# One attention output in every step, and the convolution between the second and third score tile

## Chip, cores and metric

The kernel runs on 1 core of one Trainium2 chip. Time is device microseconds of one execution; a few runs of each kernel are timed, beside runs of the kernel before on the same chip.

## The reference, cut

```python
# q, k, v: (8, 8, 576, 64); block causal attention (blocks of 64), then a gated linear unit
scores = np.where(mask, scale * (q @ k^T), -1e9)        # mask: block_i >= block_j
attn   = exp(scores - max) / (sum + 1e-9);  a = attn @ v
x      = a.transpose(0, 2, 1, 3).reshape(B, S, 512)      # (8, 576, 512)
gate   = sigmoid(causal_conv5(x, conv_w));  val = x @ w_val
out    = (gate * val) @ w_out                            # float32
# ... cut
```

Of the kernel before, what the change touches and what calls it, by code (L numbers as in the profile page):

```python
# [10 lines left out]
def kernel(  # L11
# [27 lines left out]
    B, H, S, D = q.shape  # L39
    NT = B * 4  # L40

    def mm(**kw):
        tc.keep_in_program_order(nc.tensor.matmul(**kw))  # L43
# [126 lines left out]
    def first_q(h, i):  # L170
        return 2 * i + 1 + h

    def scores(t, part):
        b, n = divmod(t, 4)
        if part == 0:
            pts[t] = ptp.tile([128, 2880], fp16, tag="pt", name="pt")
        pt = pts[t]
        hs = (slice(0, 64), slice(64, 128))
        qT = [qkT[b][hs[h], n, 0, :] for h in range(2)]
        kT = [qkT[b][hs[h], n, 1, :] for h in range(2)]  # L180

        def full(ps, h, i, lo):
            f = 64 * first_q(h, i)
            mm(out=ps[:, h, lo:lo + S - f], lhsT=kT[h][:, f - 64:f + 64], rhs=qT[h][:, f:S],
               start=True, stop=True, skip_group_check=True)

        def ex(o, src, w):
            nc.scalar.activation(out=pt[:, o:o + w], in_=src, func=AF.Exp, bias=0.0,  # L188
                                 scale=0.125)

        if part == 0:
            ps = psS.tile([128, 2, 512], fp32, tag="S")
            full(ps, 0, 0, 0)
            full(ps, 1, 0, 0)
            full(ps, 1, 3, 448)
            ex(0, ps[:, :, :], 1024)
            ps = psS.tile([128, 2, 512], fp32, tag="S")
            full(ps, 0, 1, 0)
            full(ps, 1, 1, 0)
            full(ps, 0, 3, 384)  # L200
            full(ps, 1, 2, 320)
            ex(1024, ps[:, :, :], 1024)
            return
        q4 = [x.rearrange("d (j x) -> d j x", x=64) for x in qT]
        if part == 1:
            ps = psS.tile([128, 2, 512], fp32, tag="S")
            full(ps, 0, 2, 0)
            mm(out=ps[64:128, 1, 0:256], lhsT=kT[1][:, 0:64], rhs=q4[1][:, 1:8:2, :],
               start=True, stop=True, skip_group_check=True)
            for i in range(4):  # L210
                f = 64 * (2 * i + 1)
                mm(out=ps[0:64, 1, 64 * i:64 * i + 64], lhsT=kT[1][:, f:f + 64],
                   rhs=qT[1][:, f:f + 64], start=True, stop=True, skip_group_check=True)
            nc.scalar.activation(  # L214
                out=pt[:, 2048:2560].rearrange("p (h x) -> p h x", h=2),
                in_=ps[:, :, 0:256], func=AF.Exp, bias=0.0, scale=0.125)
            return
        ps = psS.tile([128, 2, 512], fp32, tag="S")
        mm(out=ps[64:128, 0, 0:320], lhsT=kT[1][:, 0:64], rhs=q4[1][:, 0:9:2, :],
           start=True, stop=True, skip_group_check=True)  # L220
        for i in range(5):
            f = 128 * i
            mm(out=ps[0:64, 0, 64 * i:64 * i + 64], lhsT=kT[0][:, f:f + 64],
               rhs=qT[0][:, f:f + 64], start=True, stop=True, skip_group_check=True)
        ex(XO, ps[:, 0, 0:320], 320)

    def p_cols(pt, h, i, lo, hi):
        o = TOF[h][i] + 64 * (lo - first_q(h, i))
        return pt[:, o:o + 64 * (hi - lo)]
# [52 lines left out]
    def pv(t):  # L282
        b, n = divmod(t, 4)
        pt = pts.pop(t)
        v16, vd, vz = vts[b]
        xb = xbs[b % NXB]
        rb = rp.tile([128, 2, 9, 32], fp32, tag="rb")
        vec.stream_shuffle(out=rb[:, :, :, :].rearrange("p e j y -> p (e j y)"),
                                 in_=rqs[b % 2][:, :, :].rearrange("p e x -> p (e x)"),
                                 mask=[n] * 32)  # L290
        for part, (lo, hi) in enumerate(((0, 5), (5, 9))):
            nb = hi - lo
            x = psG.tile([128, nb, 64], fp32, tag="G")
            todo = []
            for h in range(2):
                hs = slice(64 * h, 64 * h + 64)
                jobs = []
                for i in range(4):
                    a = max(lo, first_q(h, i))
                    if a < hi:  # L300
                        jobs.append(dict(out=x[hs, a - lo:, :],
                                         lhsT=v16[:, 9 * n + 5 * h + i, :],
                                         rhs=p_cols(pt, h, i, a, hi)))
                if h == 1:
                    for i in range(4):
                        j = 2 * i + 1
                        if lo <= j < hi:
                            jobs.append(dict(out=x[hs, j - lo, :], lhsT=vd[:, n, i, :],
                                             rhs=pt[:, YO + 64 * i:YO + 64 * i + 64]))
                    i0, m = ((0, 3), (3, 2))[part]  # L310
                    jobs.append(dict(out=x[hs, 2 * i0 - lo:nb:2, :],
                                     lhsT=vz[:, n, 5, :],
                                     rhs=pt[:, XO + 64 * i0:XO + 64 * (i0 + m)]))
                else:
                    for i in range(5):
                        if lo <= 2 * i < hi:
                            jobs.append(dict(out=x[hs, 2 * i - lo, :],
                                             lhsT=vz[:, n, i, :],
                                             rhs=pt[:, XO + 64 * i:XO + 64 * i + 64]))
                todo.append(jobs)  # L320
            for z in range(max(len(x_) for x_ in todo)):
                for x_ in todo:
                    if z < len(x_):
                        mm(start=(z == 0), stop=(z == len(x_) - 1), skip_group_check=True,
                           **x_[z])
            vec.tensor_tensor(
                out=xb[:, n, 4 + 64 * lo:4 + 64 * hi].rearrange("p (j e y) -> p j e y", e=2, y=32),
                in0=x[:, :, :].rearrange("p j (e y) -> p j e y", e=2),
                in1=rb[:, :, lo:hi, :].rearrange("p e j y -> p j e y"),
                op=ALU.mult)  # L330
# [87 lines left out]
    for t in range(NT + LAG):  # L418
        b, r = divmod(t, 4)
        m = t - LAG  # L420
        hb = (t + 3) // 2 if t % 2 else t // 2 + 1
        tr = [(hb, part) for part in ((1, 2), (0,))[t % 2]] if hb < 2 * B else []
        if t == 0:
            tr.insert(0, (1, 0))
        if t < NT:
            scores(t, 0)
        if t % 2 == 0:
            load_pair(t // 2 + 3)
        if r == 0 and b < B:
            load_v(b)  # L430
        if t in (2, 3, 6, 7):
            weights(t // 4, t % 2 * 2)
        if r == (2 if b else 1) and b < B:
            cast_v(b)
        if t <= 4:
            conv_weights(t - 1)
        if proj:
            project(*proj.pop(0))
        if r == 0 and 1 <= b <= B:
            den(b - 1)  # L440
        if m < 0 and tr:
            trans(*tr.pop(0))
        for n in range(2):
            if r == 3 and 1 <= b <= B:
                pv(4 * b - 4 + n)
            if r == 0 and 2 <= b <= B + 1:
                pv(4 * b - 6 + n)
            if n == 0 and t < NT:
                if 0 <= m:
                    scores(t, 1)  # L450
                    scores(t, 2)
                else:
                    scores(t, 1)
                    if tr:
                        trans(*tr.pop(0))
        if m < 0 and t < NT:
            scores(t, 2)
        if r == 1 and 1 <= b <= B:
            spread(b - 1)
        if 0 <= m < NT:  # L460
            gate(*divmod(m, 4))
        if tr:
            trans(*tr.pop(0))
        if 0 <= m < NT:
            val(*divmod(m, 4))
            u, i = divmod(m, 8)
            if i == 3:
                proj.extend((u, j) for j in range(4))
            if i == 7:
                proj.extend((u, j) for j in range(4, 9))  # L470
        if tr:
            trans(*tr.pop(0))
        if proj:
            project(*proj.pop(0))
    while proj:
        project(*proj.pop(0))


# [1 line left out]
_INS = ['q', 'k', 'v', 'moe_w_val', 'moe_conv_w', 'moe_w_out']  # L480
_OUTS = [((8, 576, 512), 'float32')]
# [25 lines left out]
```

## The kernel before: what the change touches

One step `t` handles the scores of one *pair* of heads. A batch has four pairs, so four steps; step `t` is step `r = t % 4` of batch `b = t // 4`. The convolution and value product of a pair run nine steps later (`m = t - 9`).

```python
stg = ...bufs=4   # staging of loads
psS = ctx.enter_context(tc.tile_pool(name="psS", bufs=2, space=PSUM))   # score tiles
psG = ctx.enter_context(tc.tile_pool(name="psG", bufs=4, space=PSUM))   # all other small PSUM tiles
# scores(t, 0): two score tiles, exp of 128x1024 each; scores(t, 1): third, exp 128x512; scores(t, 2): fourth, exp 128x320
# den(b):   88 small matmuls -> dn, then the reciprocal on DVE
# spread(b): eight 32x288 copies of the reciprocals, on POOL (half on DVE for batch 0)
# pv(t):    shuffle on DVE, attention output matmuls -> two psG tiles x, two multiplies on DVE -> xb
# gate:     two times five matmuls -> cv, tanh on ACT;   val: two times four matmuls -> vp, multiply on DVE
# project:  four matmuls -> ot, ACT copies to ob, and ACT issues the store:
        nc.scalar.copy(out=ob[:, :], in_=ot[:, :])
        nc.scalar.dma_start(out=out2d[...], in_=ob[:, :])

    LAG = 9
    for t in range(NT + LAG):
        ...
        if t < NT:
            scores(t, 0)
        ...                                   # loads and casts
        if proj:
            project(*proj.pop(0))
        if r == 0 and 1 <= b <= B:
            den(b - 1)
        ...
        for n in range(2):
            if r == 3 and 1 <= b <= B:
                pv(4 * b - 4 + n)
            if r == 0 and 2 <= b <= B + 1:
                pv(4 * b - 6 + n)
            if n == 0 and t < NT:
                if 0 <= m:
                    scores(t, 1)
                    scores(t, 2)
                ...
        if r == 1 and 1 <= b <= B:
            spread(b - 1)
        if 0 <= m < NT:
            gate(*divmod(m, 4))
        ...                                   # transposes, val, transposes, project
```

The softmax here doesn't subtract the row's maximum and nothing guards it: scores larger than these inputs give would overflow.

## Time and profile before

| | before |
|---|---|
| time, median of 3 (range) | 264.78 us (262.64 to 264.83) |
| span of the profiled run | 261.9 us |
| PE / DVE / ACT / POOL busy | 85 / 57 / 53 / 44% |
| one steady batch | 28.09 us (29.34 us with one store more); once 34.76 us |

Lines of the page of the kernel before: busy microseconds of each engine, then busy tenths of PE and the granted TensorE clock in 40 slices of the span.

```profile
PE 222.4 (85%) x3064; PEld 153.8 (59%) x3064; DVE 149.2 (57%) x297; ACT 138.3 (53%) x233; POOL 116.0 (44%) x168
...
PE   0698986888989998997698989899989997999993
...
PEclk9997799779999999999599999999999999999999
```

PE is the engine to shorten. Past the start (the first 59 us) only one slice has a low clock (5, near 124 to 131 us). The list of PE's waits in the kernel before (total, times, longest):

```profile
PE ps L43 <- ACT pt L188: 14.5, 29, 3.6
...
PE x L43 <- DVE ri L56: 2.0, 5, 1.0
...
PE cv L43 <- DVE xb_68 L56: 1.7, 3, 0.7
PE cv L43 <- DVE xb_67 L56: 1.4, 2, 0.7
```

`ps` are the score tiles. There are two buffers; the third and fourth tile of a step wait until an exponential has emptied one. PE's timeline in one plain step of the kernel before (start, length, group, idle time before it and its releaser):

```profile
150.47 0.51 PE L43 MATMUL ps<-qkT 64*128 64x256 f16 x6
151.39 0.34 PE L43 MATMUL ps<-qkT 64*64 64x320 f16 x6 [0.41 <-ACT pt L188]
151.66 1.40 PE L43 MATMUL cv<-xb_67,diag 128*128 128x288 f16 x10
```

and around the second attention output and the convolution in the step with the denominators:

```profile
165.04 0.54 PE L43 MATMUL x<-pt,t 128*64 128x256 f16 x8 [0.27 <-DVE ri L56]
...
166.35 0.90 PE L43 MATMUL cv<-xb_67,diag 128*128 128x288 f16 x6 [0.67 <-DVE xb_68 L56]
```

The gap of 0.41 us comes back in three of the four steps of a batch, the two lower ones once per batch. What stands between the second and third tile differs: a projection alone (1.1 us from start to start, gap of 0.41 us at 88.52 us), one attention output alone (1.0 us, 0.41 us at 94.21 us), and in the denominator step the denominators with one attention output. Three batches in a row, by window of the kernel before (length, then busy time and instructions of PE, PEld, DVE, ACT, POOL, then PEclk, DMA share, GB/s):

```profile
75.41:103.50 28.09, 25.48 (x381) 17.84 (x381) 17.08 (x34) 16.26 (x28) 14.19 (x21) 1.00 0.93 277
103.50:138.26 34.76, 28.83 (x384) 19.59 (x384) 17.17 (x34) 16.90 (x29) 14.00 (x21) 0.90 0.48 142
138.26:166.35 28.09, 25.61 (x380) 17.85 (x380) 17.07 (x34) 16.29 (x28) 13.99 (x21) 1.00 0.32 81
```

The middle one is 6.7 us longer. ACT's timeline in it shows why: a store in ACT's queue (`ACTq`) is issued 3.6 us after its copy `ob` ended, and the exponentials behind it in the queue wait.

```profile
121.10 0.58 ACT L376 COPY ob<-ot 128x512 f32<-128x512 f32 x1 [2.36 <-PE ot L43]
121.58 1.03 ACT L188 ACTIVATE pt<-ps 128x1024 f16<-128x1024 f32 x1
125.32 0.34 ACTq L377 DMA_DIRECT2D out_dram<-ob  x1
125.71 1.02 ACT L188 ACTIVATE pt<-ps 128x1024 f16<-128x1024 f32 x1 [3.10 <-DMA st<-in_q_dram]
```

The compiled program says what the store waits for. It hands eight DMA semaphores out in turn, to loads and stores alike, and a new DMA waits for the last user of its semaphore. This store got one last used by a q load that was stuck behind the small-packet v load; that load was issued at 115.29 us and landed 10.0 us later, at 125.29, and the store was issued at 125.32:

```
ACT  out_0_dram<-ob_2252      [waits DMAHW2, Activation]
SP   st_2717<-in_q_dram       [waits DMAHW6, DMAHW2]
```

### The profile page before, as it was taken

The numbers are of one execution on the slowest core, as the hardware profiler recorded it, in microseconds if no ns is written. First come the engines' busy times: TensorE is split into PE (matmuls) and PEld (weight loads), VectorE is DVE, ScalarE is ACT, GpSimd is POOL, SyncE is SP. The second block draws the span as 40 slices with busy tenths as digits, with TensorE's granted clock in tenths as the row PEclk, the third lists the DMA queues.
The fourth block names the chain that finished last, engine by engine and source line by source line (L and its number), as shares of the span: only waits on it lengthen the run. The fifth ranks groups of instructions, "written<-read, shape, count | busy, mean of one in ns | idle before, by whom it ended". The sixth has DMA issues, their size and how long they took to land.

```text
span 261.9 us, 7260 instructions
## 1 busy us (share of the span) xinstructions
PE 222.4 (85%) x3064; PEld 153.8 (59%) x3064; DVE 149.2 (57%) x297; ACT 138.3 (53%) x233; POOL 116.0 (44%) x168
## 2 busy tenths in 40 slices
PE   0698986888989998997698989899989997999993
PEld 0465655656765567554475568655665566677661
DVE  2269995934693297527167257932775167458140
ACT  2558695256636655673343775266645760442533
POOL 5354973996986713943009730770029202200000
PEclk9997799779999999999599999999999999999999
DMA  6998688969479696149800290029101210230305
GB/s 196 341 280 217 213 250 215 327 196 300 148 166 348 232 271 236 40 133 282 292 3 3 85 245 14 4 83 241 62 3 40 83 41 3 83 120 4 131 32 200
DMA packets 24875, 40.33 MB, mean 154 GB/s; under 512 B 1797, under 2 KB 11013, under 8 KB 24842
## 3 DMA queue, kind: packets, MB, share of 16 engines
q1 hardware_dynamic: 19648, 30.41, 40.1%
q10 hardware_dynamic: 5194, 9.45, 9.9%
q8 instruction: 24, 0.39, 0.6%
q14 instruction: 9, 0.07, 0.1%
HBM read 30.42 MB, written 9.44 MB: 152 GB/s over the span
## 4 chain that ended last, share of the span: by engine, by line
PE 54%; ACT 16%; DVE 15%; DMA 6%; issue 4%; SPq 1%; POOL 1%; ACTq 0%; DVEq 0%
PE cv L43 14%; ACT pt L188 13%; PE ps L43 9%; PE vp L43 9%; PE ot L43 8%; PE dn L43 5%; PE tr L152 5%; PE x L43 5%; DVE ri L56 4%; DMA st<-in_q_dram 4%; DVE rb L56 4%; DVE qkT L56 3%; DMA st<-in_k_dram 2%; ACT ob L376 2%; DVE xb_68 L56 1%
## 5 line engine op out<-in xcount | busy, mean ns | idle before, releaser
L188 ACT ACTIVATE pt<-ps 128x1024 f16<-128x1024 f32 (+1 forms) x96 | 76.0, 828 | 23.3 <-PE ps L43 19.5
L56 DVE COPY qkT<-tr 128x768 f16<-128x768 f16 (+1 forms) x62 | 49.3, 837 | 52.4 <-PE tr L152 52.3
L43 PE MATMUL ps<-qkT 64*64 64x64 f16 (+10 forms) x608 | 49.8, 256 | 17.7 <-ACT pt L188 14.5
L43 PEld LDWEIGHTS <-qkT 64*64 64x64 f16 (+1 forms) x608 | 24.9, 105 | 45.2 <-issue 38.0
L348 ACT ACTIVATE th<-cv 128x288 f32<-128x288 f32 x64 | 26.2, 410 | 39.1 <-PE cv L43 37.2
L118 POOL CAST t<-st 128x1152 f16<-128x1152 f32 x30 | 34.1, 1143 | 22.5 <-issue 9.8
L56 DVE SCALAR_TENSOR_TENSOR gv<-th,vp 128x288 f16<-128x288 f32 x64 | 27.0, 447 | 26.5 <-PE vp L43 25.9
L376 ACT COPY ob<-ot 128x512 f32<-128x512 f32 x36 | 21.3, 591 | 37.4 <-PE ot L43 36.3
L43 PEld LDWEIGHTS <-diag 128*128 128x128 f16 x320 | 30.4, 100 | 14.2 <-issue 4.1
L43 PE MATMUL ot<-w_out_sb,gv 128*128 128x512 f16 x144 | 35.8, 380 | 0.5
L152 PE MATMUL tr<-ident_59,t 128*128 128x128 f16 x288 | 27.3, 240 | 7.7 <-DVE ident_59 L94 6.5
L43 PE MATMUL x<-pt,t 128*64 128x256 f16 (+3 forms) x384 | 27.9, 258 | 3.3 <-DVE ri L56 2.0
L279 POOL COPY rq_71<-ri 32x288 f32<-32x288 f32 x32 | 13.4, 420 | 35.6 <-DVE ri L56 34.4
L152 PEld LDWEIGHTS <-t 128*128 128x128 f16 x288 | 21.4, 108 | 12.0 <-DVE t L56 6.3
L279 POOL COPY rq_70<-ri 32x288 f32<-32x288 f32 x28 | 11.8, 421 | 36.2 <-DVE ri L56 35.1
L43 PEld LDWEIGHTS <-w_val_sb 128*128 128x128 f16 x256 | 24.3, 98 | 5.5
L214 ACT ACTIVATE pt<-ps 128x512 f16<-128x512 f32 x32 | 19.7, 615 | 14.0 <-PE ps L43 13.9
L43 PEld LDWEIGHTS <-t 128*64 128x64 f16 x384 | 18.9, 113 | 7.4 <-issue 5.0
L131 POOL CAST t<-st 128x2304 f16<-128x2304 f32 x8 | 16.8, 2103 | 11.8 <-DMA st<-in_v_dram 11.5
L43 PEld LDWEIGHTS <-gv 128*128 128x128 f16 x144 | 12.7, 98 | 14.7 <-issue 2.1
L56 DVE RECIPROCAL ri<-dn 128x288 f32<-128x288 f32 x8 | 15.6, 1956 | 9.9 <-PE dn L43 9.9
L43 PE MATMUL cv<-xb_67,diag 128*128 128x288 f16 x120 | 18.0, 299 | 1.7 <-DVE xb_68 L56 1.7
(55 smaller groups left out, 258.5 us busy)
## 6 DMA issues: line engine op xcount, KB each, us to landing
st<-in_q_dram SPq DMA_DIRECT2D x32, 288.0 KB, 4.9
st<-in_k_dram SPq DMA_DIRECT2D x32, 288.0 KB, 5.0
out_dram<-ob ACTq DMA_DIRECT2D x36, 256.0 KB, 2.0
st<-in_moe_w_val_dram SPq DMA_DIRECT2D x2, 512.0 KB, 6.6
st<-in_moe_w_out_dram SPq DMA_DIRECT2D x2, 512.0 KB, 5.6
st<-in_v_dram SPq DMA_DIRECT2D x8, 0.2 KB, 9.4
conv_nat<-in_moe_conv_w_dram ACTq DMA_DIRECT2D x1, 10.0 KB
```

What stands on the lines that cost most here:

```text
L43: tc.keep_in_program_order(nc.tensor.matmul(**kw))
L56: return lambda **kw: tc.keep_in_program_order(f(**kw))
L118: cast(out=t[:, :, :, :], in_=st[:, :, :, :].rearrange("p z c d -> p c z d"))
L131: nc.gpsimd.tensor_copy(out=t[:, :, :], in_=st[:, :, :])
L152: tc.keep_in_program_order(nc.tensor.transpose(out=tr[:, s, :], in_=q16[hb, w][:, c, :, :], identity=ident16[:, :]))
L188: nc.scalar.activation(out=pt[:, o:o + w], in_=src, func=AF.Exp, bias=0.0, scale=0.125)
L214: nc.scalar.activation(out=pt[:, 2048:2560].rearrange("p (h x) -> p h x", h=2), in_=ps[:, :, 0:256], func=AF.Exp, bias=0.0, scale=0.125)
L279: move.tensor_copy(out=rqs[b % 2][r0:r0 + 32, e, :], in_=ri[r1:r1 + 32, :])
L348: nc.scalar.activation(out=th[:, HF * hf:HF * hf + HF], in_=cv[:, :], func=AF.Tanh, bias=0.0, scale=0.5)
L376: nc.scalar.copy(out=ob[:, :], in_=ot[:, :])
```

## The change

The intent: give ACT enough time between the second and the third score tile, by one attention output per step in place of two in every other step, and by the convolution in between. No work is added or removed.

```diff
-        for n in range(2):
-            if r == 3 and 1 <= b <= B:
-                pv(4 * b - 4 + n)
-            if r == 0 and 2 <= b <= B + 1:
-                pv(4 * b - 6 + n)
-            if n == 0 and t < NT:
-                if 0 <= m:
-                    scores(t, 1)
-                    scores(t, 2)
-                else:
-                    scores(t, 1)
-                    if tr:
-                        trans(*tr.pop(0))
-        if m < 0 and t < NT:
+        if 0 <= t - 6 < NT:
+            pv(t - 6)
+        if m < 0:
+            scores(t, 1)
+            if tr:
+                trans(*tr.pop(0))
             scores(t, 2)
         if r == 1 and 1 <= b <= B:
             spread(b - 1)
         if 0 <= m < NT:
             gate(*divmod(m, 4))
+            if t < NT:
+                scores(t, 1)
+                scores(t, 2)
```

## The prediction

> **What bounds it now.** TensorE. The page has PE busy 222.4 of 261.9 us (85%), DVE 57%, ACT 53%; PE is 54% of the chain that ended last. In the timeline the steady stretch repeats per batch of four pairs: from the convolution after a batch's last attention output to the next, 28.09 us (75.4 to 103.5, 138.3 to 166.4), PE busy 25.5. So 2.5 us per batch are PE gaps, regular ones:
> - The third and fourth score tiles need a score buffer (there are two) that an exponential must free. Between second and third tile PE has a projection, one attention output, or nothing; ACT needs 1.8 us for two wide exponentials. PE idles about 0.2 and 0.4 us a step; the list of waits gives 14.5 us in 29 waits.
> - In the denominator step a 1.96 us reciprocal blocks DVE, and two attention outputs fill the four small PSUM buffers: gaps of 0.27 and 0.68 us.
> - Once, at 122 to 126 us, ACT sits 3.1 us: a store in its queue is issued at 125.3 though its copy ended at 121.7. The instruction listing shows that the store reuses a DMA semaphore whose previous user is a q load, itself queued behind the small-packet v load (the wait is put down to that load). PE waits 3.62 us, and the granted clock is then 0.5 until about 131 us (convolution 2.58 us, elsewhere 1.40). That batch takes 34.76 us, 6.7 over its neighbours. This agrees with the Trainium skill, "TensorE: Matmul & The Clock Gate", HAM oscillation: PE gaps over about 3.4 us bring back the half clock.
>
> **The change.** No work is added or removed. Attention outputs go from two per step in two steps of four (7 and 8 steps late) to one in every step (6 late). Convolution (1.24 us of PE from start to start) and attention output (1.05) stand between second and third score tile in every steady step, so ACT has 2.3 us and more for two exponentials. The last two are covered by value product (1.0) and transposes.
>
> **On the critical path** (sums of timeline gaps):
> 1. Score tiles waiting for exponentials after 52 us, without the stall: 8.9 us; I expect 8 gone.
> 2. Denominator steps: 1 us each; a wait of the second convolution half for the reciprocal remains (1.05 plus 0.6 against 2.0 us: 0.4). Net gain 3 us over the kernel.
> 3. The stall: DMA semaphores are handed out in another order; the ninth store now waits for a DMA landed long before. Gain 6.5 us, if no other store falls on a late load; I see none.
> 4. New: the first attention output, at step 6, directly needs the spread reciprocals (done near 37 us) while DVE is full: up to 1.5 us lost, mostly regained in steps 7 and 8. Other new waits: 1 us. The tail keeps its work.
>
> 264.8 - 8 - 3 - 6.5 + 2 = about 249 us. Range 244 to 257. Faster by over 2%: 0.93; within 2%: 0.06; slower: 0.01.
>
> **What would show it.** Score tiles waiting for exponentials down from 14.5 to under 4 us; batch period 26 us or a little less, PE busy time equal; no ACT wait over 2 us on an input load and no half clock after 60 us; in the denominator step one gap of 0.4 us before the second convolution half. Tail equal within 1 us.
>
> **What would make it wrong.** The stall comes back elsewhere, with half clock (+6). PE time that I call busy is partly waiting hidden by modelled ends, so gaps only move. The four small PSUM buffers bring waits for DVE or ACT in every step. Waits like the "issue" one of 1.97 us at 45.5 fall worse in the DMA-heavy start.

## The result, and the profile after

| | before | after |
|---|---|---|
| time, median | 264.42 us (4 runs) | 244.88 us (4 runs, one of them slow, 248.22) |
| ratio | | 0.9268, 95% interval 0.9212 to 0.9324 |
| span of the profiled run | 261.9 us | 242.9 us |
| PE busy | 222.4 us, 85% | 218.9 us, 90% |

A ratio is the mean time of one kernel's fast runs over that of the other's fast runs of the same rounds, so it is not quite the ratio of the medians. The kernel takes 7.3% less time.

The same lines of the page, after:

```profile
PE 218.9 (90%) x3064; PEld 147.1 (61%) x3064; DVE 151.6 (62%) x297; ACT 140.1 (58%) x233; POOL 116.5 (48%) x168
...
PE   0598989897699999999999999999999999999993
...
PEclk9998577999799999999999999999999999999998
```

PE's waits after:

```profile
PE vp L43 <- DVE xb_68 L56: 3.7, 1, 3.7
PE cv L43 <- DVE ri L56: 3.0, 6, 0.5
PE ps L43 <- ACT pt L188: 1.7, 6, 0.4
```

The wait for exponentials of this form fell from 14.5 to 1.7 us, all of it in the first 52 us (those of the third tile's exponential, `pt L214`, went from 0.3 to 0.8 us, also there). A plain step of the kernel after, on PE, has no gap that the view shows:

```profile
143.10 0.61 PE L43 MATMUL ps<-qkT 64*128 64x512 f16 x7
143.64 0.35 PE L43 MATMUL x<-pt,t 128*64 128x256 f16 x4
...
144.47 1.41 PE L43 MATMUL cv<-xb_67,diag 128*128 128x288 f16 x10
145.81 0.28 PE L43 MATMUL ps<-qkT 64*128 64x256 f16 x1
```

The batches by window, after; no one is long now, as no store is held (the middle one has one store more than its neighbours):

```profile
74.07:99.67 25.60, 25.02 (x380) 16.78 (x380) 17.33 (x34) 16.57 (x28) 14.05 (x20) 1.00 0.92 262
99.67:126.40 26.73, 26.06 (x384) 17.09 (x384) 17.38 (x34) 17.04 (x29) 14.10 (x20) 1.00 0.69 220
126.40:152.00 25.60, 25.02 (x380) 16.78 (x380) 17.34 (x34) 16.57 (x28) 14.10 (x20) 1.00 0.35 100
```

Two gaps are left. One is 0.50 us in the denominator step: the second half of the convolution waits for the PSUM slot of the denominators `dn`, which the reciprocal on DVE (`ri`) still reads. PE's timeline of the kernel after shows it:

```profile
125.11 0.79 PE L43 MATMUL cv<-xb_69,diag 128*128 128x288 f16 x5
126.40 0.78 PE L43 MATMUL cv<-xb_69,diag 128*128 128x288 f16 x5 [0.50 <-DVE ri L56]
```

The other, of 3.65 us at 59 us, is new (`vp` in the list of waits). It is the first attention output of batch 1. DVE's timeline after, there:

```profile
54.82 0.81 DVE L56 SCALAR_TENSOR_TENSOR gv<-th,vp 128x288 f16<-128x288 f32 x2
61.32 0.01 DVE L56 LOAD_MASK_SELECT rb<-rq_71  x1 [5.69 <-POOL rq_71 L279]
61.32 0.79 DVE L56 STREAM_SHUFFLE rb<-rq_71 128x576 f32<-128x576 f32 x1
```

DVE waits 5.69 us for POOL's spreading copies, which end at 61.3 us because casts stand before them. Half clock follows for 3.4 us.

Where the 19.0 us of span went. The first matmul of each of the eight denominators is a common mark in both PE timelines; the table has the time between marks.

| stretch | before | after | difference |
|---|---|---|---|
| start to den 0 | 27.85 | 28.08 | +0.23 |
| den 0 to 1 | 14.12 | 16.59 | +2.47 |
| 1 to 2 (new stall in after) | 28.46 | 25.74 | -2.72 |
| 2 to 3 | 28.08 | 25.60 | -2.48 |
| 3 to 4 (store stall in before) | 34.77 | 26.73 | -8.04 |
| 4 to 5 | 28.10 | 25.60 | -2.50 |
| 5 to 6 | 29.34 | 26.72 | -2.62 |
| 6 to 7 | 26.21 | 23.72 | -2.49 |
| 7 to end | 44.97 | 44.12 | -0.85 |

The start is noisy: two other kernels below that are the same program up to denominator 1 reached it at 43.73 and 44.50 us, against 41.97 in before; the kernel after, run again below, reached it at 41.80 us, against 44.67 here. So +2.47 lies within the scatter of the start. The same holds for -2.72: the second profile of the kernel after has 29.35 us there. Denominator 2 was reached at 70.41 and 71.15 us in the two profiles of after, and at 70.43, 70.82 and 73.26 us in before and those two kernels: the start as a whole shows no gain clear of its scatter. The stretch from 3 to 4 has five stores, as that from 5 to 6 has; against that neighbour the store stall costs 34.77 - 29.34 = 5.4 us.

### The profile page after: what moved, and what is told of

Read it like the earlier page. It is cut to its first block, busy times and chain, and to the rows that moved or that the text cites. A ratio compares the mean times of both kernels' runs of the same rounds, so it can differ in the third digit from the quotient of the medians.

```text
span 242.9 us, 7262 instructions
## 1 busy us (share of the span) xinstructions
PE 218.9 (90%) x3064; PEld 147.1 (61%) x3064; DVE 151.6 (62%) x297; ACT 140.1 (58%) x233; POOL 116.5 (48%) x168
## 4 chain that ended last, share of the span: by engine, by line
PE 59%; DVE 12%; DMA 12%; POOL 9%; SPq 4%; issue 2%; ACT 0%; POOLq 0%; DVEq 0%; ACTq 0%
PE cv L43 14%; PE ot L43 13%; PE vp L43 9%; PE ps L43 8%; DMA st<-in_k_dram 7%; PE x L43 7%; DVE qkT L56 5%; DVE ri L56 5%; SPq L46 4%; PE tr L152 4%; DMA st<-in_v_dram 4%; PE dn L43 4%; POOL t L118 3%; POOL rq_71 L279 1%; POOL d L135 1%
## 5 line engine op out<-in xcount | busy, mean ns | idle before, releaser
L43 PE MATMUL ps<-qkT 64*64 64x64 f16 (+10 forms) x608 | 46.2, 259 | 4.1 <-ACT pt L188 1.7
L43 PEld LDWEIGHTS <-qkT 64*64 64x64 f16 (+1 forms) x608 | 21.5, 105 | 28.9 <-issue 20.8
L43 PEld LDWEIGHTS <-diag 128*128 128x128 f16 x320 | 28.8, 98 | 12.7 <-issue 4.1
L152 PE MATMUL tr<-ident_59,t 128*128 128x128 f16 x288 | 27.8, 243 | 8.3 <-DVE ident_59 L94 7.0
L152 PEld LDWEIGHTS <-t 128*128 128x128 f16 x288 | 19.9, 108 | 13.5 <-DVE t L56 6.8
L214 ACT ACTIVATE pt<-ps 128x512 f16<-128x512 f32 x32 | 19.1, 598 | 9.3 <-PE ps L43 7.8
L43 PEld LDWEIGHTS <-t 128*64 128x64 f16 x384 | 18.4, 113 | 9.4 <-issue 7.9
L43 PEld LDWEIGHTS <-gv 128*128 128x128 f16 x144 | 12.7, 98 | 14.8 <-issue 2.1
L43 PE MATMUL cv<-xb_67,diag 128*128 128x288 f16 x120 | 17.4, 289 | 1.0 <-DVE ri L56 1.0
```

Source lines behind the costliest of these rows:

```text
L43: tc.keep_in_program_order(nc.tensor.matmul(**kw))
L152: tc.keep_in_program_order(nc.tensor.transpose(out=tr[:, s, :], in_=q16[hb, w][:, c, :, :], identity=ident16[:, :]))
L214: nc.scalar.activation(out=pt[:, 2048:2560].rearrange("p (h x) -> p h x", h=2), in_=ps[:, :, 0:256], func=AF.Exp, bias=0.0, scale=0.125)
```

## The experiments

Theory A: the plain gain is hidden exponentials, and any PE block of about 1 us between second and third tile does it. Rivals: only one of the two moves matters, or both are needed. Apart from that, the store stall and the new stall have theories of their own.

### Only the convolution moved

```diff
                 if 0 <= m:
+                    gate(*divmod(m, 4))
                     scores(t, 1)
                     scores(t, 2)
...
-        if 0 <= m < NT:
+        if 0 <= m < NT and t >= NT:
             gate(*divmod(m, 4))
```

> Kernel before, with only the convolution moved between second and third score tile; attention outputs stay in pairs in two steps of four. Theory A (any PE block of about 1 us between the tiles hides the exponentials, and pairing the attention outputs costs a second gap in the denominator step): waits of score tiles for exponentials fall under 3 us in total, the denominator step keeps gaps of about 1 us, a batch takes about 26.6 us against 28.1 before and 25.6 after. The instruction listing shows that here the ninth store reuses the DMA semaphore of the v load itself, so an ACT stall of 2 to 3 us comes back at about 120 us. No POOL stall at 59 us, as the attention outputs start as late as before. Time 252 us (248 to 257). Theory B (one attention output per step is what matters, the place of the convolution nothing): waits for exponentials stay over 8 us, time 258 us or more.

Measured: 245.98 us, ratio 0.9274 (0.9223 to 0.9325). After 52 us there is one wait for an exponential, of 1.41 us at 120 us, and it is the store stall that was expected there: the v load was issued at 110.67 us and landed 8.1 us later, at 118.77, and the ninth store, whose copy had ended at 116.32, was issued at 118.80. An earlier store was held as well, for 2.8 us until 81.76 us (the releaser is a q load): PE waits 1.83 us, and den 2 to 3 takes 27.88 us against 25.60 in after. Den 4 to 5 takes 25.89 us (before 28.10, after 25.60); there the convolution waits 0.50 us for the reciprocal and a projection 0.56 us. There is no 3.65 us stall (den 1 to 2: 23.17 us). The absent 3.65 us stall hides in the total what the two held stores cost, so that the total equals that of the kernel after is partly chance; the steady batch is the cleaner measure. There the move of the convolution alone gives 2.21 of 2.50 us, and rival B falls. But the convolution hardly ever stands alone here: a projection, an attention output or the denominators stand beside it (2.2 us from start to start at 133.02 us). In the two steps where it is alone (51.63 and 55.50 us, 1.34 us from start to start) no wait for it is listed; in the second the twelve matmuls of the third and fourth tile take 0.95 us in place of 0.64.

### Only the attention outputs moved

```diff
+            if t < NT:
+                scores(t, 1)
+                scores(t, 2)
             gate(*divmod(m, 4))
-            if t < NT:
-                scores(t, 1)
-                scores(t, 2)
```
(against the kernel after)

> Kernel after, with the convolution put back behind the fourth score tile; one attention output per step stays between second and third tile. Theory A: the attention output (1.05 us of PE) already covers the wait: the score buffer of the third tile is free about 0.5 us after the second tile, that of the fourth about 1.4 us after it. Waits for exponentials stay under 3 us; the 0.50 us gap before the second convolution half in the denominator step goes, because the score tiles then stand between; batch 25.2 to 25.8 us; the POOL stall of 3.65 us at 59 us stays. Time 243 us (240 to 247). Rival C (both blocks are needed): waits for exponentials of 0.4 us in each step without a projection, batch 26.5 us or more, time 249 us or more.

Measured: 246.21 us, ratio 0.9273 (0.9213 to 0.9332). The profiled run was the slow one (249.45 us), with 5.22 us of new stall in place of 3.65; only its steady part is used. Den 4 to 5 takes 25.72 us. The 0.50 us gap in the denominator step is gone except in the last batch, but one of 0.2 us before the value product is left there. And in the step ahead of it, where the attention output stands alone between the tiles, PE still waits for exponentials: 0.41 us in each of the last five batches, and in two of them 0.22 us more. PE's timeline of this run:

```profile
121.52 0.35 PE L43 MATMUL x<-pt,t 128*64 128x256 f16 x4
...
122.64 0.51 PE L43 MATMUL ps<-qkT 64*128 64x256 f16 x6 [0.22 <-ACT pt L188]
123.56 0.34 PE L43 MATMUL ps<-qkT 64*64 64x320 f16 x6 [0.41 <-ACT pt L188]
```

In the two steps where a projection stands there too (1.80 us from start to start at 108.06 us) there is no gap. Rival C falls for the time: each move alone gives nearly the whole steady gain, and the gains don't add. Theory A falls too as it was worded. A block of 1.0 us alone leaves 0.41 us, here and in the kernel before; the convolution's 1.34 us alone leaves 0.3 us at most, and 1.8 us and more leaves none. One move was enough because most steps already had another block in that place.

### The store stall: another semaphore

```diff
         nc.scalar.dma_start(out=out2d[...], in_=ob[:, :])
+        if (u, j) == (0, 7):
+            nc.scalar.dma_start(out=spare[0:1, 0:64], in_=ob[0:1, 0:64])
```
(against the kernel before)

> Kernel before, with one store of 256 bytes into an unused tile added behind the eighth output store, so that the ninth reuses the DMA semaphore of the eighth store and no longer that of the late q load. Theory: the ACT wait of 3.1 us and the PE wait of 3.6 us at 122 to 126 us and the half clock after them go, the batch falls from 34.8 to 29.3 us, time 264.4 - 5.4 = 259 us (257.5 to 260.5), ratio 0.980. Rival (the ACT store issue is late because the DMA rings are full of small v packets, not because of the semaphore): the stall stays, time 264.

Measured: 264.25 us, ratio 0.9966 (0.9904 to 1.0027): no gain. But the wait is another one. ACT's timeline of this run:

```profile
121.48 0.58 ACT L377 COPY ob<-ot 128x512 f32<-128x512 f32 x1 [1.95 <-PE ot L43]
...
125.00 0.40 ACTq L378 DMA_DIRECT2D out_dram<-ob  x1
125.44 1.02 ACT L189 ACTIVATE pt<-ps 128x1024 f16<-128x1024 f32 x1 [2.45 <-DMA out_dram<-ob]
```

The releaser is now the eighth store (`out_dram<-ob`), whose semaphore the ninth got, and that store had landed late as well (issued at 117.46 us, 7.5 us to landing, against a median of 2.0 us over the kernel before), at 124.96 us; the ninth was issued at 125.00. So the run misses: I had picked a semaphore whose user was late too, and it doesn't tell the theories apart by time. The change of the releaser speaks for the semaphore.

### The store stall: the store from another queue

```diff
-        nc.scalar.dma_start(out=out2d[...], in_=ob[:, :])
+        q = nc.gpsimd if (u, j) == (0, 8) else nc.scalar
+        q.dma_start(out=out2d[...], in_=ob[:, :])
```
(against the kernel before)

> Kernel before, with only the ninth output store issued from POOL's queue in place of ACT's. The run with the spare store left the stall, but its releaser changed from the q load to the eighth store, as the semaphore given to the ninth store did. Theory: the stall is ACT's queue held by that one store; with the store elsewhere ACT goes on, the PE wait of 3.6 us and the half clock go, the batch falls from 34.8 to 29.3 us and the time by 5.4 us, ratio 0.980 (0.975 to 0.985). Rival (ACT is held by something else in that stretch, instruction fetch or full rings): stall stays, ratio 1.0.

Measured: 260.13 us, ratio 0.9790 (0.9738 to 0.9843). ACT's timeline in that step:

```profile
124.11 0.58 ACT L376 COPY ob<-ot 128x512 f32<-128x512 f32 x1 [2.35 <-PE ot L43]
124.59 1.95 ACT L188 ACTIVATE pt<-ps 128x1024 f16<-128x1024 f32 x2
```

Both exponentials run in one piece, the PE gap is the usual 0.41 us, there is no half clock there, and den 3 to 4 takes 29.53 us. So one held store cost the kernel before 2.1%, about 5.5 us (a gain clear of the noise; whether it is over 2% the interval leaves open). That it was the semaphore and not full rings is shown by three kernels in which the ninth store's semaphore had three different last users: a q load (before), the v load (only the convolution moved) and the eighth store (spare store). In each the store was issued within 0.1 us of that DMA's landing. In the kernel after the last user, by the compiled program, was a k load issued by 100.2 us, and the ninth store was issued at 118.22 us, while loads issued from 112.66 us on were under way, without a wait.

### The new stall: spreading of batch 1 on DVE

```diff
-                    move = vec if b == 0 and h == 0 else nc.gpsimd
+                    move = vec if b == 1 or b == 0 and h == 0 else nc.gpsimd
```
(against the kernel after)

> Kernel after, with the eight spreading copies of batch 1 on DVE in place of POOL, no other change. Theory: the PE stall of 3.65 us at 59 us and the half clock of 3.4 us after it go, because DVE no longer waits 5.7 us for POOL, which is behind with casts; the time between second and third denominators falls from 25.7 to about 21.5 us, total 240.5 us (239 to 242.5). Rival (the loads bound this stretch, so the wait only moves to the next casts): under 1.5 us gained, 243.5 us or more.

Measured: 245.62 us, ratio 0.9286 (0.9234 to 0.9338): no gain, den 1 to 2 25.98 us. PE now waits 4.19 us for DVE. The chain of waits in this run shows DVE's copies, and POOL's timeline the casts beside them:

```profile
52.70 0.45 DVE rq L56
53.15 0.01 issue
53.16 1.11 DVE rq L56
54.27 0.01 issue
54.29 1.15 DVE rq L56
```

```profile
53.07 1.04 POOL L400 TENSOR_SCALAR w_out_sb<-st 128x1024 f16<-128x1024 f32 x1
54.06 2.38 POOL L118 CAST t<-st 128x1152 f16<-128x1152 f32 x2
```

Three of the eight copies, which take 0.30 to 0.45 us otherwise, grow to 1.11 to 1.15 us, about the length of one of POOL's operations beside them (1.04 us, and two in 2.38 us); the eight take 5.3 us. The Trainium skill, "SBUF — State Buffer", section "Who interferes with whom", says that VectorE in a 2-port mode and GpSimd lock each other out of a shared port for a whole instruction. These lengths agree; which mode the copies ran in, no view shows. My theory that the stall would go was wrong, and so was the rival: no load bounds the stretch, DVE itself does.

### The new stall: less POOL work before the spreading

```diff
-        if t in (2, 3, 6, 7):
-            weights(t // 4, t % 2 * 2)
+        if t in (2, 3, 10, 11):
+            weights(t // 10, t % 2 * 2)
...
-                    move = vec if b == 0 and h == 0 else nc.gpsimd
+                    move = vec if b <= 1 and h == 0 else nc.gpsimd
```
(against the kernel after)

> Kernel after, with the two w_out casts four steps later and half of the spreading copies of batch 1 on DVE (four there, four on POOL). All eight on DVE took 5.3 us there beside POOL's casts and PE still waited 4.2 us. Theory (the spreading of batch 1 is the late thing, by about 3.6 us): PE gaps at 58 to 63 us under 1 us, no half clock after them, second to third denominators 22 us (21 to 23.5) against 25.7, time 241.5 us (239.5 to 244). Rival (loads bound the start, any gain there is given back at the next cast): third denominators still at 69 us or later, time 244 or more.

Measured: 240.80 us, ratio 0.9080 (0.9046 to 0.9115). The gap is 0.53 us, no half clock follows, den 1 to 2 takes 22.31 us, den 2 lies at 65.97 us. The gain is kept to the end, so nothing in the loads takes it back.

### The 0.50 us gap: denominators behind the fourth score tile

```diff
-        if r == 0 and 1 <= b <= B:
+        if r == 0 and 1 <= b <= 2:
             den(b - 1)
...
                 scores(t, 1)
                 scores(t, 2)
+        if r == 0 and 3 <= b <= B:
+            den(b - 1)
```
(against the kernel after; `e8_both` is this edit and the one above together)

> Kernel after, with the denominators of batches 2 to 7 put behind the fourth score tile, so that the second convolution half no longer waits for the reciprocal. Theory (the 0.50 us gap is a small-PSUM slot held by the reciprocal): the six gaps of 0.50 us go, batch 25.6 to about 25.0 us, total 3 to 4 us less than after's 244.9: 241.5 (239.5 to 244). Rival (the slot is only waited for elsewhere: a transpose or value product waits instead): batch stays within 0.2 us of 25.6, time 244 to 246.

> The two edits on the kernel after together (denominators late from batch 2, early spreading of batch 1). Theory: the gains add, 238 us (235.5 to 241), ratio to before 0.90. Rival (no sum): within 1 us of the better of the two.

Measured: 248.18 us, ratio 0.9360 (0.9320 to 0.9400), and 245.74 us, ratio 0.9255 (0.9207 to 0.9303), for both edits. The place costs: den 4 to 5 26.31 us against 25.60. PE's timeline:

```profile
130.86 0.49 PE L152 MATMUL tr<-ident,t 128*128 128x128 f16 x6 [0.63 <-DVE ri L56]
132.01 1.04 PE L43 MATMUL ot<-w_out_sb,gv 128*128 128x512 f16 x4 [0.65 <-DVE qkT L56]
```

The reciprocal (1.96 us) now stands in DVE's queue ahead of the copies that must free the next slots, and two gaps of 0.63 and 0.65 us take the place of one of 0.50. The rival had the direction. With both edits the sum of a gain and a loss is met, neither the sum of two gains nor the better of the two.

### The 0.50 us gap: denominators behind the attention output

```diff
             pv(t - 6)
+        if r == 0 and 3 <= b <= B:
+            den(b - 1)
```
(against the early spreading kernel, with the first place kept for `b <= 2`)

The kernel after and the early spreading kernel ran again beside it on the same chip.

> The kernel after, unchanged, on the same chip as the two beside it. About 245 us, ratio to before 0.926.

> The kernel with the early spreading of batch 1 again, on the same chip: 241 us, 1.5% under the kernel after, ratio 0.908.

> The early spreading kernel with the denominators of batches 2 to 7 put behind the attention output of their step, ahead of the convolution (behind the fourth score tile they cost 0.7 us per batch). Theory (DVE's order and the small PSUM slots decide: the reciprocal must come behind the attention output's multiplies, and 2.4 us of PE must follow the denominators before their slot is used again; here convolution 1.24, score tiles 0.85 and transposes 0.35 follow): the 0.50 us gaps go and no other comes, batch 25.6 to about 25.0 us, time 237 us (235 to 239.5). Rival (as with the later place, the transposes behind the reciprocal wait instead): batch 25.6 us or more, 240.5 us or more.

| same chip, 5 rounds | median us | ratio to before | 95% interval |
|---|---|---|---|
| kernel after | 245.11 | 0.9228 | 0.9193 to 0.9262 |
| early spreading | 242.31 | 0.9127 | 0.9088 to 0.9165 |
| and denominators behind the attention output | 237.81 | 0.8951 | 0.8910 to 0.8991 |

Early spreading gained less than the first time: its profiled run had a gap of 2.83 us at 57 us where the first had 0.53, and PE stood 1.06 us with no releaser shown at 98 us, so the kernel still scatters, and that kernel's gain over the kernel after lies between 1 and 2%. The last kernel's PE timeline in the denominator step:

```profile
119.04 1.61 PE L43 MATMUL dn<-pt,oh 128*32 128x160 f16 x88
120.58 1.40 PE L43 MATMUL cv<-xb,diag 128*128 128x288 f16 x10
121.91 0.64 PE L43 MATMUL ps<-qkT 64*128 64x256 f16 x12
122.48 0.51 PE L152 MATMUL tr<-ident,t 128*128 128x128 f16 x6
```

There is no gap; den 4 to 5 takes 24.93 us, 0.67 less than in the kernel after. This version beats both kernels: 10.5% under before, and 3.0% under after by the ratio of the two ratios, 0.8951 / 0.9228. Every result above was correct against the reference.

## Why the prediction was right, and where its sum was off

The time (244.88 us, predicted 249 with 244 to 257) lies in the range, 0.9 us above its lower end: the mechanisms of the two main terms were right, their sizes were not. Point by point:

1. *Waits for exponentials go.* Right: 9.1 us of them after 52 us (12.7 with the stall, less 3.6) fell to none. The prediction gave ACT 2.3 us and more, with both blocks in between. That fits: 1.0 us alone leaves 0.41 us, 1.8 us leaves none. It named the blocks that stood there already, but did not say that beside them either move would give most of the gain.
2. *Denominator step: one gap of 0.4 us stays before the second convolution half.* Right: 0.50 us, in that place.
3. *What these gaps are worth was mis-sized.* I took 8 + 3 = 11 us, the length of the gaps. The batches lost 2.5 us each, five of them 12.7 us with the regular part of the long one (34.77 - 26.73 - 5.4 = 2.6), and the tail 0.9. In one clean batch the shown gaps fell by 2.48 - 0.58 = 1.90 us, and PE busy time with the same 380 matmuls fell from 25.61 to 25.02 us besides. The prediction called busy time equal. A likely reason, not tested: a single score matmul is shown as 0.28 us long, while twelve in a row take 0.64 us together, so each gap leaves the shown length of the matmul before it uncovered, and part of what a gap costs is counted as busy. The Trainium skill, "Perfetto Trace Analysis", section "Identifying the Most-Contended Engine", warns that matmul busy time is a poor measure of how near a kernel is to its peak, because pipelined matmuls look smaller in the trace; this agrees, by 0.59 us a batch.
4. *The store stall goes: 6.5 us.* The mechanism was right; the kernel with that one store elsewhere confirms it at 2.1%. The size was 5.4 us: I had measured the long batch against a neighbour with fewer stores.
5. *A new stall at the first attention output, step 6, of up to 1.5 us.* Wrong place and size: step 6 has a gap under 0.6 us. The stall is at step 10, batch 1, 3.65 us and 4.92 us in two profiles, with half clock behind it. I had looked only at when batch 0's reciprocals are spread, not at POOL's queue before those of batch 1. Over the whole start nothing is lost or gained clear of its scatter: denominator 2 comes at 70.41 and 71.15 us, at 70.43 in before. Against the first run with early spreading the stall costs 25.74 - 22.31 = 3.4 us in this stretch.
6. *No half clock after 60 us.* Missed with the stall: it lies at 63.4 to 66.8 us. *Tail equal within 1 us*: it is 0.9 us shorter.

The sum by the table: -13.6 (batches and tail) - 5.4 (store) - 0.0 (start, where the new stall and the scatter of the start cancel) = -19.0 us, where I had -11 - 6.5 + 2 = -15.5.

The Trainium skill, "Perfetto Trace Analysis", section "Optimization Strategy" under "Identifying Performance Opportunities", says that consistent bubbles can mean too little PSUM for the next tile. That reading would have asked for a third score buffer. Here the bubble went with the same buffers, by work that needs none of them placed between; a third buffer was not tried.

## What to carry to other kernels

When a producer waits for a buffer that another engine empties, put independent work as long as that emptying between fill and refill, and count what stands there already: here 1.0 us left a gap of 0.41 us, 1.8 us left none, and more hardly added to the gain. Before moving work earlier, look at the queue of every engine that feeds it, at the first time it is needed and not only in the steady state. A DMA issued from an engine's queue can hold that engine for an unrelated late load; find what the issue waits for before explaining a lone long gap by the engine's own work.

## What the Trainium skill lacked or had wrong

- "TensorE: Matmul & The Clock Gate", section on HAM oscillation, gives PE-idle gaps over about 3.4 us as what brings back the half clock. Gaps of 3.62 to 5.22 us did so here (3.4 or 6.8 us of half clock), but so did one shown as 2.96 us (6.8 us), in the run with the spare store; one of 2.83 us did not. In the start of the kernel before, half clock ran from 53.0 to 56.6 us with no single gap over 0.64 us in the five us before. So 3.4 us of one gap is no sharp limit here.
- No page that I read says that a DMA issue can hold its engine because the program gives it a semaphore whose last user is a late load. Here it held ACT for 3.10 us and cost 2.1% of the kernel.
- "Perfetto Trace Analysis" says that pipelined matmuls look smaller in the trace, but not by how much when gaps are closed: here 0.59 us of 25.61 us busy went with the gaps, so a gap was worth about 1.3 times its shown length (2.49 / 1.90).
